# Linear attention and a gated convolution feed-forward: a new order of instructions, with two convolutions moved to VectorE and one addition made by a transfer

## The chip, the cores and the metric

The kernel runs on one core of a Trainium2 chip. The metric is the device time of one execution in microseconds. The engines are TensorE (PE, with its weight loads PEld), VectorE (DVE), ScalarE (ACT), GpSimd (POOL) and SyncE (SP). Each has its own instruction queue, which runs in order, and they meet in semaphores. Loads are issued by POOL, SP and ACT and carried out by 16 DMA engines.

## The reference, cut to what matters

For 8 batches, 8 heads, 576 positions and head size 64:

```
kv   = k^T v                            # per head, 64 x 64
o    = q kv
x    = o / sqrt(mean(o^2) + 1e-6) * g   # per head; heads side by side: x is 576 x 512
h    = max(x w_in, 0)                   # 576 x 1024
c    = w[0] * h[s-1] + w[1] * h[s] + w[2] * h[s+1]   # along the sequence, per channel
out  = (h * sigmoid(c)) w_out           # 576 x 512, fp32
```

All inputs are fp32. The kernel works in bf16 with fp32 accumulation.

## The kernel before, in words

The kernel is one list of tokens, `ORDER`. Each token names a small operation and its arguments, and behind `@` the buffers that it takes: a PSUM bank (0 to 7, two neighbours for most), or a slot of a ring in SBUF. A loop at the end runs the tokens in turn, and a last pass ties every instruction to the one before it on its engine. So the list fixes, for each engine, the order of all its work; a token that waits holds up everything behind it on the same engine. The list was written out by a planner, with costs for the operations.

Tokens by engine, with arguments `b` (batch), `u` (half of the heads, 4 each), `s` (half of the sequence), `f` (one of 8 groups of 128 hidden channels):

- Loads: `pre` brings batch 0's q, k, v in fp32 into staging buffers, by SP and ACT, in the order of `HEAD`. All other loads are on POOL's queue and cast to bf16 on the way: `Li` (w_in), `Lo` (w_out), `Lq`, `Lk`, `Lv` (one batch, or half of one where the last argument is 2). `gt` makes POOL wait for one staged tile of k before the first of them. q has three slots, k and v two; a load into a slot waits for the last reader of the batch that had it.
- Head: `cad` and `caa` cast the staged tiles on DVE and ACT; `ps`, `pl`, `pn`, `pg`, `pc`, `dg` and `ct` make constants (a spreading matrix, a selection matrix, the scaled convolution weights, and diagonal matrices of them). `fi` issues unread products of zeros on TensorE, `n` of `w` columns.
- Attention: `kv` (k^T v, L402; for batches 6 and 7 `kz`, L479), its copy `kva` on ACT or `kvd` on DVE; `qt` (transposes of q, L433) and the copies `qa`, `qd`; `ot` (q kv, L460); `sq` (squares, ACT), `on` or `oq` (sums over a head with a matrix of ones: `on` in whole matmuls, `oq` in quarters), `nl` (1/sqrt, ACT), `mo` (the scaled x, DVE). Batches 4 to 7 take another way: `oc`, `ss`, `ln`, `sl`, `sp`, `mu`; batches 6 and 7 have q transposed by DMA (`tq`).
- Hidden layer: `hk` (in two parts, L658), `hs` (L628) and `hm` (L613) multiply x by w_in; `rp`, `rh` and `re` apply the maximum with zero on ACT.
- Convolution and gate: `ta` scales a channel group by the outer two weights into the buffer `taps` (two `TENSOR_SCALAR`, L681 and L682, one written one element further right), `aa` adds the two with their shifts (L687), `ab` adds h (L692), all on DVE; the middle weight has been divided out and comes back as the scale of `sg`, the sigmoid on ACT (L698). `mg` multiplies h by it (DVE, L722). The second argument is the number of batches handled at once, the third a pair of channel groups `j` (f = 2j and 2j + 1). There are two `taps` buffers. For four channel groups of batch 0 (f = 0 to 3) TensorE makes the convolution instead: `cv` is six matmuls with the identity and two diagonal matrices from `dg` (L708), and `sc` the sigmoid from PSUM (L715).
- Output: `om` multiplies h by w_out for 128 rows of a pair of batches (L732, in two parts of four matmuls), `ea` (ACT, L738) or `ed` (DVE, L743) copies the row block out of PSUM and `st` stores it (SP, L748). The last block goes in two halves (`oh`, `eh`, `sh`).

Batches go in pairs through the convolution and the output product: pair p has batches 2p and 2p + 1.

Of the kernel before, what the change touches and what calls it, by code (L numbers as in the profile page):

```python
# [64 lines left out]
sq.0.1.1@3 oq.0.0.1@0 nl.0.0.1@2 fi.1.512@4 fi.1.512@4 hk.0.1.0.0@4 hk.0.1.0.1 rp.1.0@0 on.0.1.1@0 nl.0.1.1@3
hk.0.2.0.0@5 hk.0.2.0.1 rp.2.0 dg.3 mo.0.0.1 dg.2 hk.0.3.0.0@4 hk.0.3.0.1 hk.0.0.0.0@2 hk.0.0.0.1 rp.0.0 hk.0.0.1.0@3
rp.3.0 hk.0.1.1.0@5 hk.0.3.1.0@0 mo.0.1.1 hk.0.3.1.1 rp.3.1 hk.0.1.1.1 rp.1.1 hk.0.0.1.1 rp.0.1 dg.0 hk.0.2.1.0@1
hk.0.2.1.1 qt.1.0.0@6 kv.1.0.1@4 rp.2.1 cv.0.2@2 sc.0.2@0 cv.0.3@0 qd.1.0.0@2 kvd.1.0.1@1 ot.1.0.1@6 sc.0.3 pl
sq.1.0.1@4 cv.0.1@4 cv.0.0@2 Lq.1.2.2 Lk.1.2.2 Lv.1.2.2 sc.0.1@1 fi.2.512@0 qt.1.1.0@0 qd.1.1.0@3 mg.0.1.1 Lo.0.8
sc.0.0 mg.0.1.0 oq.1.0.1@4 nl.1.0.1@4 mo.1.0.1@1 fi.1.512@2 hk.0.5.1.0@2 hk.0.5.0.0@3 hk.0.5.0.1 rp.5.0 hk.0.5.1.1  # L70
rp.5.1 ta.0.1.5@0 hk.0.4.1.0@0 hk.0.4.1.1 rp.4.1 hk.0.7.0.0@1 hk.0.7.0.1 kv.1.1.1@4 kvd.1.1.1 rp.7.0 ot.1.0.0@2
sq.1.0.0@5 hk.0.7.1.0@6 hk.0.7.1.1 rp.7.1 ta.0.1.7@1 ot.1.1.1@0 sq.1.1.1@6 oq.1.0.0@4 nl.1.0.0@5 mo.1.0.0 hk.0.4.0.0@6
hk.0.4.0.1 rp.4.0 hk.0.6.1.0@7 hk.0.6.1.1 rp.6.1 oq.1.1.1@4 nl.1.1.1@6 mo.1.1.1 hk.0.6.0.0@6 Lq.2.0.4@2 hk.0.6.0.1
rp.6.0 ta.0.1.4 hk.1.6.1.0@7 ta.0.1.6 hk.1.0.1.0@2 ot.1.1.0@4 sq.1.1.0@7 aa.0.1.2 hk.1.1.1.0@3 hk.1.2.1.0@6 hk.1.6.1.1
# [5 lines left out]
Lq.3.0.4@0 Lk.3.0.4@0 Lv.3.0.4@1 Lq.4.0.4@1 aa.1.1.0 hk.1.4.0.0@3 om.0.1.0.4@2 rh.1.4.1 hk.1.4.0.1 rh.1.4.0  # L80
om.0.2.0.4@5 kv.2.0.2@6 mg.0.1.3 om.0.1.4.4 ab.1.1.0 sg.1.1.0 sg.1.1.1 kvd.2.0.2@2 ot.2.0.1@0 sq.2.0.1@0 ed.0.1@0
st.0.1 qt.3.1.0@6 qd.3.1.0@1 Lk.4.0.4@1 Lv.4.0.4@0 Lq.5.0.4@2 om.0.2.4.4 on.2.0.1@2 qt.3.0.0@6 qd.3.0.0@2 nl.2.0.1@8
mo.2.0.1@2 om.0.3.0.4@4 ea.0.2@1 ot.2.1.1@6 ot.2.1.0@2 mg.1.1.0 om.0.3.4.4 ed.0.3@2 sq.2.1.0@1 sq.2.1.1@2 on.2.1.0@0
nl.2.1.0@9 mo.2.1.0 om.0.0.0.4@5 hk.1.3.0.0@4 on.2.1.1@0 st.0.2 nl.2.1.1@0 mo.2.1.1 om.0.0.4.4 ed.0.0@3 ot.2.0.0@2
# [46 lines left out]
mg.7.1.3 om.3.3.0.4@2 om.3.3.4.4 ed.3.3@5 st.3.3 mg.7.1.2 om.3.1.0.4@1 om.3.2.0.4@7 om.3.0.4.4 om.3.2.4.4 ed.3.2@0  # L131
st.3.2 ed.3.0@2 st.3.0 om.3.1.4.4 ea.3.1@1 st.3.1 om.3.4.0.4@0 om.3.5.0.4@4 om.3.6.0.4@3 om.3.7.0.4@6 om.3.7.4.4
ed.3.7@4 om.3.5.4.4 ea.3.5@3 st.3.5 om.3.4.4.4 ed.3.4@5 st.3.4 st.3.7 om.3.6.4.4 ea.3.6@0 st.3.6 oh.3.8.1@1 eh.3.8.1@2
sh.3.8.1 oh.3.8.0@0 eh.3.8.0@1 sh.3.8.0
"""


@with_exitstack
def kernel(
# [79 lines left out]
    def bank():  # L219
        return banks[:, slots.pop(0), :]  # L220
# [604 lines left out]
```

## Time and profile before

| what | value |
|---|---|
| median of 3 runs | 177.75 us (177.67 to 177.93) |
| span of the profiled execution | 175.6 us |
| median of the runs less that span | 2.15 us |
| PE busy | 167.9 us (96%) |
| DVE busy | 149.5 us (85%) |
| ACT busy | 148.9 us (85%) |
| POOL busy | 22.2 us (13%) |
| moved by DMA | 29.11 MB |

The profiled execution is told by its span, from its first to its last instruction; of its own time nothing else is given, so the table sets the span beside the median of the runs. Some time before and after the span belongs to a run as well. The page lists busy times by engine, forty slices of the span with the busy share of each engine, the chain of work that ended last, and groups of instructions by source line. A landing time is counted from the issue of a transfer.

### The profile page before, as it was taken

The numbers are of one execution on the slowest core, as the hardware profiler recorded it, in microseconds if no ns is written. First come the engines' busy times: TensorE is split into PE (matmuls) and PEld (weight loads), VectorE is DVE, ScalarE is ACT, GpSimd is POOL, SyncE is SP. The second block draws the span as 40 slices with busy tenths as digits, with TensorE's granted clock in tenths as the row PEclk, the third lists the DMA queues.
The fourth block names the chain that finished last, engine by engine and source line by source line (L and its number), as shares of the span: only waits on it lengthen the run. The fifth ranks groups of instructions, "written<-read, shape, count | busy, mean of one in ns | idle before, by whom it ended". The sixth has DMA issues, their size and how long they took to land.

```text
span 175.6 us, 5070 instructions
## 1 busy us (share of the span) xinstructions
PE 167.9 (96%) x2097; PEld 100.0 (57%) x2114; DVE 149.5 (85%) x290; ACT 148.9 (85%) x268; POOL 22.2 (13%) x35
## 2 busy tenths in 40 slices
PE   7979999999999999999999999999999999999992
PEld 2334766676447677644467764444877744444451
DVE  2796638899688899999999998989999999999950
ACT  2368899999978999999999998999999967676721
POOL 3094512200603013030000000000000000000000
PEclk9999999999999999999999999999999999999999
DMA  5999999999999999999999050330310003064486
GB/s 159 392 323 207 207 207 207 208 208 209 207 241 230 227 207 207 170 182 197 258 181 161 14 134 0 119 123 0 119 63 0 0 0 116 13 239 175 179 304 237
DMA packets 25911, 29.11 MB, mean 166 GB/s; under 512 B 6036, under 2 KB 20384, under 8 KB 25888
## 3 DMA queue, kind: packets, MB, share of 16 engines
q0 software_dynamic: 13296, 14.50, 49.2%
q1 hardware_dynamic: 12048, 13.11, 26.2%
q10 hardware_dynamic: 544, 1.18, 1.7%
q8 instruction: 16, 0.26, 0.6%
q14 instruction: 7, 0.06, 0.1%
HBM read 32.52 MB, written 9.44 MB: 239 GB/s over the span
## 4 chain that ended last, share of the span: by engine, by line
PE 76%; DVE 12%; ACT 5%; DMA 3%; issue 3%; ACTq 0%; DVEq 0%
PE banks L732 32%; PE banks L628 14%; PE banks L613 9%; PE banks L658 4%; DMA stg<-in_v_dram 3%; PE banks L460 3%; DVE h L722 2%; PE banks L708 2%; ACT taps L698 2%; PE banks L402 2%; PE banks L593 2%; PE banks L433 1%; PE banks L528 1%; DVE taps L681 1%; PE banks L286 1%
## 5 line engine op out<-in xcount | busy, mean ns | idle before, releaser
L732 PE MATMUL banks<-w_out_sb,h 128*128 128x512 bf16 x267 | 62.8, 379 | 1.2 <-issue 0.6
L698 ACT ACTIVATE taps<-taps,cw 128x576 bf16<-128x576 bf16 (+1 forms) x44 | 40.6, 958 | 5.7 <-DVE taps L692 5.5
L732 PEld LDWEIGHTS <-h 128*128 128x128 bf16 x280 | 26.2, 98 | 30.0 <-issue 1.1
L628 PE MATMUL banks<-x,w_in_sb 128*128 128x288 bf16 (+2 forms) x256 | 34.2, 286 | 0.0
L640 ACT ACTIVATE h<-banks 128x288 bf16<-128x288 f32 (+2 forms) x80 | 29.5, 460 | 0.3 <-PE banks L658 0.2
L628 PEld LDWEIGHTS <-w_in_sb 128*128 128x128 bf16 x256 | 24.4, 98 | 7.8 <-issue 0.8
L722 DVE TENSOR_TENSOR h<-h,taps 128x1152 bf16<-128x1152 bf16 (+1 forms) x24 | 22.8, 952 | 1.2 <-ACT taps L698 1.2
L687 DVE TENSOR_TENSOR taps<-taps 128x1152 bf16<-128x1152 bf16 (+1 forms) x22 | 21.5, 978 | 0.5
L509 ACT ACTIVATE sq<-banks 128x576 bf16<-128x576 f32 (+2 forms) x32 | 20.8, 691 | 1.1 <-PE banks L460 1.1
L692 DVE TENSOR_TENSOR taps<-taps,h 128x1152 bf16<-128x1152 bf16 (+1 forms) x22 | 21.4, 972 | 0.3
L681 DVE TENSOR_SCALAR taps<-h,cw 128x576 bf16<-128x576 bf16 (+1 forms) x44 | 18.7, 424 | 0.6 <-ACT h L665 0.5
L682 DVE TENSOR_SCALAR taps<-h,cw 128x576 bf16<-128x576 bf16 (+1 forms) x44 | 18.4, 418 | 0.0
L738 ACT ACTIVATE row<-banks 128x512 f32<-128x512 f32 x23 | 13.5, 597 | 5.7 <-PE banks L732 4.2
L658 PE MATMUL banks<-x,w_in_sb 128*128 128x288 bf16 (+2 forms) x128 | 17.7, 286 | 0.1
L613 PE MATMUL banks<-x,w_in_sb 128*128 128x288 bf16 x128 | 16.9, 286 | 0.0
L556 DVE SCALAR_TENSOR_TENSOR x<-banks,cw,rs 128x576 bf16<-128x576 f32 (+2 forms) x16 | 13.0, 816 | 3.9 <-ACT rs L545 3.6
L658 PEld LDWEIGHTS <-w_in_sb 128*128 128x128 bf16 x128 | 12.0, 98 | 4.4 <-issue 0.5
L227 ACT ACT_TABLE_LOAD x10 | 12.8, 1283 | 2.0 <-issue 1.8
L613 PEld LDWEIGHTS <-w_in_sb 128*128 128x128 bf16 x128 | 12.3, 98 | 3.7 <-issue 0.2
L443 DVE COPY qT<-banks 128x1152 bf16<-128x1152 bf16 (+2 forms) x13 | 8.8, 681 | 5.7 <-PE banks L433 5.7
L545 ACT ACTIVATE rs<-banks,eps_sb 128x576 f32<-128x576 f32 (+2 forms) x16 | 11.8, 740 | 1.1 <-PE banks L528 1.1
L599 DVE SCALAR_TENSOR_TENSOR x<-o,cw,banks 128x576 bf16<-128x576 f32 (+2 forms) x16 | 12.1, 810 | 0.7 <-PE banks L593 0.5
(89 smaller groups left out, 162.9 us busy)
## 6 DMA issues: line engine op xcount, KB each, us to landing
out_dram<-row SPq DMA_DIRECT2D x35, 256.0 KB, 2.3
q_sb<-in_q_dram POOLq DMA_DIRECT2D x6, 576.0 KB, 17.9
k_sb<-in_k_dram POOLq DMA_DIRECT2D x6, 576.0 KB, 14.5
v_sb<-in_v_dram POOLq DMA_DIRECT2D x6, 576.0 KB, 17.9
stg<-in_v_dram ACTq DMA_DIRECT2D x2, 576.0 KB, 6.2
stg<-in_k_dram SPq DMA_DIRECT2D x4, 288.0 KB, 6.9
w_in_sb<-in_moe_w_in_dram POOLq DMA_DIRECT2D x2, 512.0 KB, 9.9
w_out_sb<-in_moe_w_out_dram POOLq DMA_DIRECT2D x1, 1024.0 KB, 15.5
```

Source lines behind the costliest of these rows:

```text
L509: nc.scalar.activation(T["sq", b, u, s], T["o", b, u, s], AX.Square)
L613: nc.tensor.matmul(ps[:, s, :HS], w_in_sb[:, t, f * P:(f + 1) * P], T["x", b][:, t, c0:c1], start=(t == 0), stop=(t == NT - 1))
L628: nc.tensor.matmul(ps, w_in_sb[:, t, f * P:(f + 1) * P], T["x", b][:, t, c0:c1], start=(t == 0), stop=(t == NT - 1))
L640: nc.scalar.activation(h, fr, AX.Relu)
L658: nc.tensor.matmul(T[at], w_in_sb[:, t, f * P:(f + 1) * P], T["x", b][:, t, c0:c1], start=(t == 0), stop=(t == NT - 1))
L681: nc.vector.tensor_scalar_mul(tap[:, 0, f % 2, :n, 8:8 + S], h[:, f], cw[:, f:f + 1])
L682: nc.vector.tensor_scalar_mul(tap[:, 1, f % 2, :n, :S], h[:, f], cw[:, 2 * NF + f:2 * NF + f + 1])
L687: nc.vector.tensor_add(tap[:, 1, :, :n, :S], tap[:, 0, :, :n, 7:7 + S], tap[:, 1, :, :n, 1:1 + S])
L692: nc.vector.tensor_add(y, y, span(b, n)[:, 2 * j:2 * j + 2])
L698: nc.scalar.activation(y, y, AX.Sigmoid, scale=cw[:, NF + f:NF + f + 1])
L722: nc.vector.tensor_mul(h, h, tap_of(b, j)[:, 1, :, :n, :S])
L732: nc.tensor.matmul(T["om", p, m], h[:, f, m * P:(m + 1) * P], w_out_sb[:, f, :], start=(f == 0), stop=(f == NF - 1))
```

## The change

The whole list `ORDER` is replaced by another. What differs in it, and in the functions:

- Two of the four `cv`, for f = 2 and 3 of batch 0, are gone with their `sc` and the builds `dg.2` and `dg.3`; the same channel groups go by `ta.0.1.2`, `ta.0.1.3`, `aa.0.1.1`, `ab.0.1.1`, `sg.0.1.2`, `sg.0.1.3`.
- `ad.4.2.2` takes the place of `aa.4.2.2` (batches 4 and 5, channel groups 4 and 5): a transfer issued by POOL adds the second tap to the first in place, so the sum stands in the other half of the buffer, at column 7. `y_of` hands that place to `ab`, `sg` and `mg`, and `mg` then sets the padding column to zero again.
- The unread products of the start are now `ff`, in fp32 (9 of 256 columns, and five of 128, 192 or 256 behind or between them), with fewer and narrower `fi` behind them.
- The head: four casts go from DVE to ACT (eight are on ACT, four on DVE), `pn`, `pl`, `ps` come early, `HEAD` brings k of the last heads ahead of `q.1.0`, and w_in is loaded in three parts instead of two.
- POOL's loads stand in another order: all of w_in first, then batch 1, batch 2, w_out, batch 3, then q4, k4, q5, v4, v5, q6, k5, v6, q7, k6, v7, k7. Before it was: half of w_in, half of batch 1, the rest of w_in, the rest of batch 1, w_out, batch 2, batch 3, q4, k4, v4, q5, q6, k5, v5, q7, k6, v6, k7, v7.
- Five `on` become `oq`, three `kvd` become `kva` and one `kva` a `kvd`, one `qd` becomes `qa`; six `ed` become `ea` and six `ea` become `ed`, and one `eh` becomes `dh`.
- Work of all engines is put in other places, and into other banks and slots: `kv.4.0.2`, for one, stands ahead of eight `hs` and three `qt` that it used to follow.

The functions that are new or changed, and the parts of the new list that this text speaks of:

```diff
+... Lv.1.0.2@1 ... Lq.1.0.2@1 ... Lk.1.0.2@0 ... Lq.1.2.2 ... Lv.1.2.2 ... Lk.1.2.2
+... Lq.2.0.4@0 ... Lk.2.0.4@1 ... Lv.2.0.4@0 ... Lo.0.8 ... Lq.3.0.4@2 ... Lv.3.0.4@1 ... Lk.3.0.4@0 ... Lq.4.0.4@1
+... kv.2.0.2@6 hk.1.7.0.1 om.0.1.0.4@2 Lk.4.0.4@1 ... Lq.5.0.4@0 ... Lv.4.0.4@0 ...
+hs.2.7.1@2 nl.3.1.0@1 hs.2.6.0@3 mo.3.1.0 kv.4.0.2@4 qt.4.0.0@6 kvd.4.0.2@0 qt.5.0.0@0 sg.1.1.5 Lv.6.0.4@0 qd.4.0.0@0
...
+    def pair(n):
+        if 2 * n <= 512:
+            return bank()[:, :2 * n].rearrange("p (e n) -> p e n", e=2)
+        return bank2()[:, :, :n]
...
-    HEAD = (("sync", "q.0.0 k.0.1 k.1.1 q.1.0 k.2.1 k.3.1 q.0.1 q.1.1"), ("scalar", "v.0.2 v.2.2"))
+    HEAD = (("sync", "q.0.0 k.0.1 k.1.1 k.2.1 k.3.1 q.1.0 q.0.1 q.1.1"), ("scalar", "v.0.2 v.2.2"))
...
+    @op
+    def ff(n, w):
+        ps, z = bank(), zero.bitcast(FP32)
+        for _ in range(n):
+            nc.tensor.matmul(ps[:, :w], z[:, :P], z[:, :w], start=True, stop=True)
...
     def on(b, u, s):
-        ps = T["on", b, u, s] = bank2()[:, :, :c1 - c0]
+        ps = T["on", b, u, s] = pair(c1 - c0)
...
+    @op
+    def ad(b, n, j):
+        tap = tap_of(b, j)
+        T["y", b, j] = tap[:, 0, :, :n, 7:7 + S]
+        nc.gpsimd.dma_start(out=T["y", b, j], in_=tap[:, 1, :, :n, 1:1 + S], accum_op=AL.add)
+
+    def y_of(b, n, j):
+        if ("y", b, j) not in T:
+            T["y", b, j] = tap_of(b, j)[:, 1, :, :n, :S]
+        return T["y", b, j]
...
     def mg(b, n, j):
         h = span(b, n)[:, 2 * j:2 * j + 2]
-        nc.vector.tensor_mul(h, h, tap_of(b, j)[:, 1, :, :n, :S])
+        nc.vector.tensor_mul(h, h, y_of(b, n, j))
+        if ADS & {(b, j)}:
+            nc.vector.memset(tap_of(b, j)[:, 0, :, :n, 7:8], 0.0)
```

More of the change, by code (lines that the diff above doesn't have):

```diff
@@ L65 @@
[L65 to L74, printed above, removed]
@@ L80 @@
[L80 to L84, printed above, removed]
@@ L408, in kvc @@
     def kvc(eng, b, u0, n):
-        if u0 == 0:
+        if ("kvb", b) not in T:
             T["kvb", b] = ring("kvb", [P, 2, 2 * D], BF16, "kvb")
@@ L437, in qc @@
     def qc(eng, b, u, s):
-        if s == 0:
+        if ("qT", b, u) not in T:
             T["qT", b, u] = ring("qT", [P, 2, S], BF16, "qT")
```

141 lines of the change are left out of this document (78 added, 63 removed).

## The prediction

> **What bounds the kernel now.** I read the page first: busy shares, slices, chain.
>
> ```profile
> span 175.6 us, 5070 instructions
> ...
> PE 167.9 (96%) x2097; PEld 100.0 (57%) x2114; DVE 149.5 (85%) x290; ACT 148.9 (85%) x268; POOL 22.2 (13%) x35
> ...
> DMA  5999999999999999999999050330310003064486
> GB/s 159 392 323 207 207 207 207 208 208 209 207 241 230 227 207 207 170 182 197 258 181 161 14 134 0 119 123 0 119 63 0 0 0 116 13 239 175 179 304 237
> ...
> PE 76%; DVE 12%; ACT 5%; DMA 3%; issue 3%; ACTq 0%; DVEq 0%
> ```
>
> TensorE is busy for 96% and carries 76% of the chain, so at first sight less TensorE work is less time. But the DMA row shows a second full resource: the 16 engines are at nine tenths or more from slice 2 to slice 22 (4.4 to about 92 us), at a flat 207 GB/s through most of it. That is the stream of loads that also casts q, k, v and both weights to bf16, all issued on POOL. [...]
>
> Next I asked for the stretches, then the issue and landing of single loads.
>
> ```profile
> 12.90:27.10 14.20, 13.57 (x245) 8.83 (x247) 7.98 (x25) 12.95 (x23) 5.55 (x8) 1.00 1.22 207
> ...
> 32.40:40.90 8.50, 8.50 (x139) 6.50 (x137) 7.90 (x16) 8.09 (x18) 0.00 (x0) 1.00 1.21 208
> ```
>
> (Columns: window, length, busy time and count of PE, PEld, DVE, ACT, POOL, granted clock, DMA, GB/s.) The rate is the same in both, and ACT is busy for 8.09 of 8.50 us in the second.
>
> The w_out load, then v of batch 2, q of batch 3, v of batch 4 and q of batch 5, each with its issue time (after the durations) and its time to landing:
>
> ```profile
> L365 POOL DMA_DIRECT2D w_out_sb<-in_moe_w_out_dram x1: 912/912/912, 16.9 to 16.9; - x1
> ...
> DMA to landing us min/median/max: 15.5/15.5/15.5
> ```
>
> ```profile
> L347 POOL DMA_DIRECT2D v_sb<-in_v_dram x1: 740/740/740, 20.8 to 20.8; - x1
> ...
> DMA to landing us min/median/max: 20.1/20.1/20.1
> ```
>
> ```profile
> L347 POOL DMA_DIRECT2D q_sb<-in_q_dram x1: 740/740/740, 23.7 to 23.7; - x1
> ...
> DMA to landing us min/median/max: 20.1/20.1/20.1
> ```
>
> ```profile
> L347 POOL DMA_DIRECT2D v_sb<-in_v_dram x1: 760/760/760, 45.0 to 45.0; - x1
> ...
> DMA to landing us min/median/max: 15.2/15.2/15.2
> ```
>
> ```profile
> L347 POOL DMA_DIRECT2D q_sb<-in_q_dram x1: 770/770/770, 45.7 to 45.7; - x1
> ...
> DMA to landing us min/median/max: 17.3/17.3/17.3
> ```
>
> Landings: w_out 32.4, v2 40.9, q3 43.8, v4 60.2, q5 63.0. They come in the order of issue. One whole-batch load takes 2.85 us of the stream (40.9 to 43.8; 60.2 to 63.0). Between v2 and v4 lie six loads (q3, k3, v3, q4, k4, v4) and the stores of three output rows:
>
> ```profile
> 45.67 7.92 SPq L748 DMA_DIRECT2D out_dram<-row  x3
> ```
>
> 19.3 us less 6 x 2.85 leaves 2.2 us, 0.72 us a row. Now who uses these loads, from TensorE's timeline:
>
> ```profile
> 16.86 0.60 PE L658 MATMUL banks<-x,w_in_sb 128*128 128x256 bf16 x4
> ...
> 41.10 1.03 PE L732 MATMUL banks<-w_out_sb,h 128*128 128x512 bf16 x3
> ```
>
> ```profile
> 63.57 0.80 PE L433 MATMUL banks<-ident,q_sb 64*64 64x64 bf16 x72
> 64.30 2.62 PE L628 MATMUL banks<-x,w_in_sb 128*128 128x288 bf16 x20
> 66.86 0.78 PE L402 MATMUL banks<-v_sb,k_sb 64*64 64x64 bf16 x72
> 67.56 4.13 PE L628 MATMUL banks<-x,w_in_sb 128*128 128x288 bf16 x32
> ```
>
> The first hidden product (`hk`) starts at 16.9, the first output product (`om.0.1`) at 41.1, 8.7 us after w_out; batch 4's k'v (`kv.4.0.2`) at 66.9, 6.7 us after v4; `qt.5.0.0` (in the 72 transposes at 63.6) only about 1 us after q5. So no load stops TensorE before, though some are close.
>
> **The change part by part.** Prices of TensorE work, from the chain in order of time:
>
> ```profile
> 22.05 1.59 PE banks L708 x12
> ...
> 25.47 0.22 PE banks L286
> ...
> 122.98 2.94 PE banks L628 x24
> ```
>
> Two convolutions cost 1.59 us, an unread 512-column product 0.22, one hidden half-product (`hs`, four matmuls) 2.94/6 = 0.49; a `qt` of a whole unit (36 transposes) is half of 64.30 - 63.57, 0.36; a whole `kv` is 67.56 - 66.86, 0.70.
>
> *Head.* The order of the fp32 head loads (k before q.1.0), four casts moved from DVE to ACT, the fp32 unread products and the new places of `ps`, `pn`, `pl`, `pc` all act before the first `hk`. Two casts no longer wait behind `ps` on DVE, but `q.1.0` comes two transfers later. Bounds for the first `hk`: 1 us earlier (both gains kept) to 2 us later; I take 0.4 earlier, 16.4, since the chain there already alternates between casts and their users and only one link shortens. An unread product of the head in the cold stage:
>
> ```profile
> 1.20 4.45 PE L286 MATMUL banks<-zero 128*128 128x512 bf16 x10 [1.20 <-DVE zero L265]
> ...
> 5.83 2.12 PE L286 MATMUL banks<-zero 128*128 128x512 bf16 x9
> ```
>
> 10 take 4.45 us (0.43 each), later 9 take 2.12 (0.22): the array starts at half rate, though the granted clock reads 1.00. [...] If it stays slow one stretch longer, the head loses up to 2 us, which is the late bound. [...]
>
> *First `hk` to first `om`.* Before it takes 41.1 - 16.9 = 24.2 us. Gone are two convolutions (1.59) and three unread products (0.65); `kv.2.0.2` and half an `hk` are moved ahead of the `om` (0.95). That gives 22.95 us, so TensorE could start `om.0.1` at 39.4. VectorE gets the two convolutions instead (four `ta`, `aa`, `ab`), about 2.5 us:
>
> ```profile
> L687 DVE TENSOR_TENSOR taps<-taps 128x1152 bf16<-128x1152 bf16 x14 | 10.6, 759 | 0.3
> L692 DVE TENSOR_TENSOR taps<-taps,h 128x1152 bf16<-128x1152 bf16 x14 | 10.5, 753 | 0.1
> L681 DVE TENSOR_SCALAR taps<-h,cw 128x576 bf16<-128x576 bf16 x28 | 10.4, 373 | 0.6 <-ACT h L665 0.5
> ```
>
> DVE is busy 7.98 of 14.2 us in the window 12.9 to 27.1, and four `dg` builds of diagonals go, so this is covered there. ScalarE keeps its count (two `sc` become two `sg`).
>
> *But the loads.* POOL's order changes: q, k, v of batch 2 now stand ahead of w_out. The set of bytes up to w_out is then the one that before ended with v2, so w_out lands at 40.9 instead of 32.4, and `om.0.1` waits from 39.4 to 40.9. The whole gain so far is gone: it starts 0.2 earlier than before. A first `hk` anywhere up to 17.9 gives the same, so the head's bounds don't reach the end.
>
> *First `om` to `kv.4`.* Before this takes 66.9 - 41.1 = 25.8 us. In the new order eight `hs` (3.9) and three `qt` of batches 4 and 5 (1.1) stand behind `kv.4`, one `hs` (0.5) and the 0.95 above ahead: 25.8 - 5.0 - 0.95 + 0.5 = 20.3. TensorE would reach `kv.4.0.2` at 61.2. But q5 now stands ahead of v4 in POOL's order, and four output rows are stored early instead of three. v4: 40.9 + 7 x 2.85 + 4 x 0.72 = 63.7. Bounds: 63.0 (fourth row hidden) and 64.5 (loads that the POOL issues later). TensorE is in order: behind `kv.4` stand the `qt` and `hs` that it used to run there; DVE's next is the copy `kvd.4`, ACT has only a few sigmoids. I take a wait of 2.5 us, to 63.7.
>
> *After `kv.4`.* It starts 3.2 us earlier than before (66.9 to 63.7), but 5.0 - 0.5 = 4.5 us of TensorE work that used to be done is still to do: +1.3 us. After this point nothing of TensorE's work is removed. The copies of output rows: six `ed` become `ea` and six `ea` become `ed`, an even trade between DVE and ACT. I put it at 0, bounds -0.8 and +1.5, because DVE and ACT are both busy nearly all the time there (4.65 and 4.92 of 5 us in the row below), so that small shifts can open or close gaps of TensorE:
>
> ```profile
> 125.00:130.00 5.00, 5.00 (x45) 3.83 (x44) 4.65 (x6) 4.92 (x12) 0.00 (x0) 1.00 0.42 157
> ```
>
> *The accumulating transfer.* It replaces one of these on DVE and adds a small memset; the next addition then reads and writes at column 7:
>
> ```profile
> L687 DVE TENSOR_TENSOR taps<-taps 128x2304 bf16<-128x2304 bf16 x8 | 10.9, 1361 | 0.2
> L692 DVE TENSOR_TENSOR taps<-taps,h 128x2304 bf16<-128x2304 bf16 x8 | 10.8, 1355 | 0.2
> ```
>
> DVE saves 1.3 us. No row shows such a transfer: from below a 256 KB store (2.3 us), from above a 576 KB load in the full stream (17.9):
>
> ```profile
> out_dram<-row SPq DMA_DIRECT2D x35, 256.0 KB, 2.3
> q_sb<-in_q_dram POOLq DMA_DIRECT2D x6, 576.0 KB, 17.9
> ```
>
> Around 105 us the engines are almost idle, so nearer the store: about 6 us for 576 KB read twice and written once. Between `ad` and the `ab.4.2.2` that needs it DVE has `mg`, two `ta`, `aa`, `ab` and two `ed`, about 7 us. So 0; were it the upper end, DVE would stop some 10 us with `sl.6` behind it. The aligned and the odd addition cost 1355 and 1361 ns: odd reads are free. [...]
>
> **Sum.** 0 (head) + 0 (first `om`, absorbed) - 3.2 + 4.5 + 0 + 0 = +1.3 us: span 176.9. The page gives the span alone; the median 177.75 stands 2.15 us above it, which I carry over: 179.05, say 179.0.
>
> **Rivals.**
> *The loads are not the bound* (faster). If w_out and v4 are there in time, TensorE starts `om` at 39.4 and `kv.4` at 59.7: 7.2 earlier, 4.5 more to do, -2.7: 175.1. With v4 alone early, `kv.4` at 61.2, -1.2: 176.6. It decides at v4 landing at 62.4 (66.9 - 4.5): earlier is faster. For it: margins of 1 us are usual in this kernel, and my 63.7 is only 1.3 above. Against: the flat 207 GB/s and landings in order of issue.
> *The wait is made good* (no change). The stop lets ACT finish sigmoids, and later gaps of DVE, spared 1.3 us, close by about 1 us: 177.8.
> *More waits than this one* (slower still). ACT has nine `rh` and four `sg` more behind `kv.4` than before, one `ea` and one `eh` fewer:
>
> ```profile
> L698 ACT ACTIVATE taps<-taps,cw 128x576 bf16<-128x576 bf16 x28 | 20.7, 777 | 5.6 <-DVE taps L692 5.5
> ...
> L640 ACT ACTIVATE h<-banks 128x288 bf16<-128x288 f32 x48 | 17.1, 428 | 0.2 <-PE banks L658 0.2
> ...
> L738 ACT ACTIVATE row<-banks 128x512 f32<-128x512 f32 x23 | 13.5, 597 | 5.7 <-PE banks L732 4.2 <-issue 1.4
> ```
>
> 9 x 0.43 + 4 x 0.78 - 2 x 0.6 is 5.8 us, 1.3 more than TensorE's 4.5; with the transfer late by as much, 2.5 us more: 181.5. For it: ACT's full windows; against: a stopped TensorE lets ACT work ahead on sigmoids that are ready.
>
> **How the numbers follow.** Forecast (v4's wait decides, 178.2 to 180.3) 0.55; more waits 0.20; made good 0.08; faster 0.17. Within 0.2% (about what can be told from no change) means 177.4 to 178.1. Faster 0.17, same 0.08, slower 0.75. The range leaves out the clearly faster end (0.12) and the worst (0.08): 176.9 to 181.8. The forecast's own range is 178.2 to 180.3.
>
> **What would show it.** The DMA row still full to slice 21; w_out landing near 40.9 and v4 near 63.7; in the waits, TensorE (PEld L402) for `v_sb` of some 2 us and for `w_out_sb` of about 1 us, which the page before lacks; DVE's `kvd` late with it. The first `hk` near 16.4 and L708 at half its count. `ab.4.2.2` not waiting for the transfer. Wrong if v4 lands before 62.4, or if TensorE comes to `kv.4` after 64 for other reasons.

## The result, and the profile after

The changed kernel takes 182.43 us (median of 4 runs, 181.89 to 184.29) against 177.84 for the kernel before on the same chip: 1.0271 times the time, with a 95% interval from 1.0219 to 1.0323. The forecast was 179.0. The profiled execution took 181.89 with a span of 180.1, so 1.8 us lie around the span (2.15 before). The executions of several kernels with long stops of TensorE scatter by 2 us and more (181.89 to 184.29 here, 181.04 to 187.41 in e9 below), the long ones mostly at a lower mean TensorE clock (184.29 at 0.991 here, 185.87 to 187.41 at 0.97 to 0.98 in e9), so profiles at a mean clock of 1.00 are compared where this matters.

The page of the changed kernel:

```profile
span 180.1 us, 5092 instructions
...
PE 168.5 (94%) x2111; PEld 102.1 (57%) x2111; DVE 149.2 (83%) x286; ACT 153.0 (85%) x274; POOL 24.2 (13%) x37
...
PE   7799988999799995999999999999999999999992
...
DMA  5999999999999999999999204883110003435334
...
q8 instruction: 16, 0.26, 0.6%
...
PE 74%; ACT 13%; issue 4%; DVE 4%; DMA 3%; POOL 0%; ACTq 0%; DVEq 0%; POOLq 0%
```

TensorE has no less work, ACT has 4 us more and 13% of the chain instead of 5%. The PE row has a hole that the one before did not: a 5 in the sixteenth slice (67.5 to 72 us). The row `q8 instruction` was on the page before too, and I had not read it: 16 packets of 16 KB of instructions. I take them to be TensorE's: its 2111 weight loads and 2111 products make some 264 a packet, and in the seven kernels below that give TensorE 56 to 260 instructions more the row has 17 packets, in all others 16.

The landings of w_out and of batch 4's v (issue time behind the durations, then time to landing):

```profile
L377 POOL DMA_DIRECT2D w_out_sb<-in_moe_w_out_dram x1: 884/884/884, 21.9 to 21.9; - x1
...
DMA to landing us min/median/max: 19.2/19.2/19.2
```

```profile
L359 POOL DMA_DIRECT2D v_sb<-in_v_dram x1: 770/770/770, 44.4 to 44.4; - x1
...
DMA to landing us min/median/max: 19.7/19.7/19.7
```

They land at 41.1 and 64.1 (forecast 40.9 and 63.7). But TensorE waits for neither. Its timeline at the steps of the prediction (start, duration, operation; in brackets the idle time before and what ended it):

```profile
16.66 1.05 PE L670 MATMUL banks<-x,w_in_sb 128*128 128x256 bf16 x8
...
42.87 2.75 PE L757 MATMUL banks<-w_out_sb,h 128*128 128x512 bf16 x12
...
45.70 0.59 PE L445 MATMUL banks<-ident,q_sb 64*64 64x64 bf16 x49
47.52 0.38 PE L445 MATMUL banks<-ident,q_sb 64*64 64x64 bf16 x23 [1.24 <-issue]
...
64.67 0.78 PE L414 MATMUL banks<-v_sb,k_sb 64*64 64x64 bf16 x72
65.26 0.84 PE L445 MATMUL banks<-ident,q_sb 64*64 64x64 bf16 x72
66.03 2.38 PE L640 MATMUL banks<-x,w_in_sb 128*128 128x288 bf16 x18
70.52 1.89 PE L640 MATMUL banks<-x,w_in_sb 128*128 128x288 bf16 x14 [2.11 <-issue]
```

The first `hk` comes at 16.66, the first `om` at 42.87 (41.10 before), `kv.4` at 64.67 (66.86 before). Twice TensorE stops in the middle of an operation: 49 transposes into a pair of `qt` of 36 each, and 18 products into a row of `hs`, the fifth of which has done two of its four products. A bank that is not ready would stop an operation at its first instruction, not there; and the other half of x, which the third product of an `hs` is the first to read, VectorE had finished by 65.3. "issue" means that the profile shows nothing it waited for. The kernel before has no such stop of a quarter microsecond or more.

So `kv.4` comes 2.2 us earlier, 4.5 us of moved work stand behind it (eight `hs` and three `qt` more, one `hs` fewer, at the prices of the prediction), and there is a stop of 2.1 us: 4.4 of the 4.5 us by which the span grew.

### The profile page after: what moved, and what is told of

Its sections match the earlier page's. It is cut to its first block, busy times and chain, and to the rows that moved or that the text cites. A ratio compares the mean times of both kernels' runs of the same rounds, so it can differ in the third digit from the quotient of the medians.

```text
span 180.1 us, 5092 instructions
## 1 busy us (share of the span) xinstructions
PE 168.5 (94%) x2111; PEld 102.1 (57%) x2111; DVE 149.2 (83%) x286; ACT 153.0 (85%) x274; POOL 24.2 (13%) x37
## 4 chain that ended last, share of the span: by engine, by line
PE 74%; ACT 13%; issue 4%; DVE 4%; DMA 3%; POOL 0%; ACTq 0%; DVEq 0%; POOLq 0%
PE banks L757 30%; PE banks L640 15%; PE banks L625 9%; PE banks L670 7%; DMA cw_rows<-in_g_norm_dram 3%; ACT sq L521 3%; ACT L232 3%; PE banks L472 2%; ACT rs L557 2%; PE banks L445 2%; PE banks L549 2%; PE banks L414 2%; ACT h L652 2%; DVE x L611 1%; ACT h L677 1%
## 5 line engine op out<-in xcount | busy, mean ns | idle before, releaser
L757 PE MATMUL banks<-w_out_sb,h 128*128 128x512 bf16 x280 | 64.2, 379 | 0.0
L721 ACT ACTIVATE taps<-taps,cw 128x576 bf16<-128x576 bf16 (+1 forms) x46 | 42.6, 953 | 3.5 <-DVE taps L715 3.5
L640 PE MATMUL banks<-x,w_in_sb 128*128 128x288 bf16 (+2 forms) x256 | 34.5, 286 | 2.1 <-issue 2.1
L640 PEld LDWEIGHTS <-w_in_sb 128*128 128x128 bf16 x256 | 24.1, 98 | 10.6 <-issue 3.5
L715 DVE TENSOR_TENSOR taps<-taps,h 128x1152 bf16<-128x1152 bf16 (+1 forms) x23 | 22.1, 961 | 0.3
L699 DVE TENSOR_TENSOR taps<-taps 128x1152 bf16<-128x1152 bf16 (+1 forms) x22 | 20.9, 948 | 0.4
L521 ACT ACTIVATE sq<-banks 128x576 bf16<-128x576 f32 (+2 forms) x32 | 20.2, 669 | 1.0 <-PE banks L472 1.0
L693 DVE TENSOR_SCALAR taps<-h,cw 128x576 bf16<-128x576 bf16 (+1 forms) x46 | 19.3, 419 | 1.7 <-ACT h L677 1.3
L694 DVE TENSOR_SCALAR taps<-h,cw 128x576 bf16<-128x576 bf16 (+1 forms) x46 | 19.6, 427 | 0.0
L670 PE MATMUL banks<-x,w_in_sb 128*128 128x288 bf16 (+2 forms) x128 | 18.2, 287 | 0.0
L625 PEld LDWEIGHTS <-w_in_sb 128*128 128x128 bf16 x128 | 12.2, 98 | 4.6 <-issue 0.7
L557 ACT ACTIVATE rs<-banks,eps_sb 128x576 f32<-128x576 f32 (+2 forms) x16 | 11.9, 743 | 3.1 <-DVE taps L693 1.2
L670 PEld LDWEIGHTS <-w_in_sb 128*128 128x128 bf16 x128 | 11.6, 98 | 4.7 <-issue 1.4
L768 DVE COPY row<-banks 128x512 f32<-128x512 f32 x12 | 8.2, 685 | 4.7 <-PE banks L757 4.6
```

Of the source, the lines that this page charges most:

```text
L521: nc.scalar.activation(T["sq", b, u, s], T["o", b, u, s], AX.Square)
L625: nc.tensor.matmul(ps[:, s, :HS], w_in_sb[:, t, f * P:(f + 1) * P], T["x", b][:, t, c0:c1], start=(t == 0), stop=(t == NT - 1))
L640: nc.tensor.matmul(ps, w_in_sb[:, t, f * P:(f + 1) * P], T["x", b][:, t, c0:c1], start=(t == 0), stop=(t == NT - 1))
L670: nc.tensor.matmul(T[at], w_in_sb[:, t, f * P:(f + 1) * P], T["x", b][:, t, c0:c1], start=(t == 0), stop=(t == NT - 1))
L693: nc.vector.tensor_scalar_mul(tap[:, 0, f % 2, :n, 8:8 + S], h[:, f], cw[:, f:f + 1])
L694: nc.vector.tensor_scalar_mul(tap[:, 1, f % 2, :n, :S], h[:, f], cw[:, 2 * NF + f:2 * NF + f + 1])
```

## The experiments

Two theories for the stops were set against each other. A: TensorE runs out of instructions. They come in blocks through a DMA queue of their own (q8 on the page, 16 packets of 16 KB), beside the full stream of loads, and a block of short instructions is used up before the next is there. B: the stops come from data, banks or other engines in the new order. Other questions were whether the loads hold TensorE as forecast, and what the two named parts do alone. The kernels are called by the first part of their labels, e1 to e16.

### More short instructions in the kernel before (e1, e2)

`fk.n` is a new token: n unread products of zeros, 64 by 64, so two short instructions each.

```diff
-fi.9.512@0
+fi.4.512@0 fk.104@0
```

> The kernel before, with five of nine unread 512-column products of the cold head replaced by 104 unread 64x64 products, so that TensorE has about 198 more short instructions and the same work there. Their results are read by nobody. Theory A (the two stops in mid-operation, 1.24 us at 46.3 and 2.11 us at 68.4 of the changed kernel, are TensorE waiting for its own instructions, which come in blocks by a DMA queue that the full load stream slows down): the same short, dense work now meets block borders as the changed kernel's does, so stops of about 2 us open near 47 and near 67 us, and the kernel before gets 2 to 4 us slower. Rival B (the stops come from data, banks or engines of the changed order): nothing moves, within 0.5 us.

Measured: 1.0338 times the kernel before (1.0281 to 1.0396), 184.3 us. The stops in its TensorE timeline:

```profile
13.75 0.32 PE L409 MATMUL banks<-v_sb,k_sb 64*64 64x64 bf16 x16 [0.94 <-issue]
...
49.36 0.28 PE L440 MATMUL banks<-ident,q_sb 64*64 64x64 bf16 x10 [1.06 <-issue]
...
72.03 0.35 PE L409 MATMUL banks<-v_sb,k_sb 64*64 64x64 bf16 x21 [2.03 <-issue]
...
82.07 0.59 PE L409 MATMUL banks<-v_sb,k_sb 64*64 64x64 bf16 x49 [1.55 <-issue]
```

Two of them stand near the places foretold, 2.4 and 5 us later and 1.06 and 2.03 us long; two more came beside them. Nothing of the order behind the head was touched: the old order gets the same kind of stops once its instructions are counted from another start. Between the last two the trace holds 127 matmuls and 127 weight loads, so some 256 instructions, one packet. That distance comes back below (126 and 128 in e3, 127 and 128 in e16). The stops add up to 5.6 of the 7.9 us by which this span grew; the clock granted from 72 to 82 us was 0.83, and 32 products of `hs` took 5.77 us there (4.09 in e3).

The control had 56 instructions more:

```diff
-fi.9.512@0
+fi.7.512@0 fk.30@0
```

> The control of the other: two of the nine unread products become 30 short ones, 56 more instructions. Both theories: no stop opens (theory A: the block borders then fall into slower stretches, total stops about 0.1 us), time within 0.5 us of the kernel before. If this one gets slower too, it is the short products in the head, not the place of the borders.

Measured: 180.88 us, 1.0141 (1.0095 to 1.0187). The expectation failed: two stops opened, one of them in the head, where I had not worked out where the borders fall.

```profile
16.05 0.46 PE L467 MATMUL banks<-qT,kvb 64*64 64x320 bf16 x5 [0.72 <-issue]
...
79.24 0.60 PE L739 MATMUL banks<-w_out_sb,h 128*128 128x512 bf16 x2 [0.56 <-issue]
```

They are of the kind that A calls for and in mid-operation, but this run shows that A foretells the place of a stop better than its absence. With its 1.3 us of stops it accounts for less than half of the 3.3 us by which this span grew; of the rest, 1.5 us arose at the very end, where copies of rows waited for stores.

What settles the place is the count of weight loads ahead of each stop. The profile of the changed kernel up to its second stop, and that of the old order without two convolutions (e5 below) up to its stop in the middle of `kv.4` (TensorE and its weight loads are the first two counts):

```profile
0.00:70.00 70.00, 62.75 (x1117) 40.87 (x1117) 53.15 (x133) 60.06 (x113) 19.67 (x32) 1.00 1.16 229
```

```profile
0.00:70.00 70.00, 63.58 (x1109) 39.11 (x1117) 53.21 (x137) 56.80 (x108) 19.31 (x31) 1.00 1.15 228
```

| weight loads before the stop | kernels |
|---|---|
| 223 | e1, e2, e9, e12 |
| 734 | changed, e4, e7, e8, e10, e14 |
| 862 | e1 |
| 1117 | changed, e4, e5, e7, e8, e10, e11, e13, e14 |
| 1245 | e1, e3, e9, e12, e16 |
| 1372 or 1373 | e1, e2, e3, e10, e12, e13, e16 |

These are all the stops that the profiles put down to "issue" and that last 0.4 us or more, with those of e7, e10 and e13 that bear VectorE's name (below) and three shorter ones at the same counts. The counts lie 128 apart, or multiples of that to within one, in both orders, whatever operation stands there and whatever data come when. Theory B gives no reason for that.

### Short instructions in the quiet and in the stream (e15, e16)

The sharpest test of A came last. The same 130 short products, once at 100 us, where the loads are over, and once at 72 us.

```diff
-om.1.2.0.4@2
+fk.130@2 om.1.2.0.4@2
```

> The kernel before with 260 short unread instructions (130 products of 64x64, 2.1 us of TensorE by the 82 that took 1.32 us in an earlier run) ahead of om.1.2.0.4 at 100 us, where the loads are over. If the stops come from the instruction supply behind a full load stream: at most a small stop here (under 1 us), span 2 to 3 us longer. If a block of 256 short instructions stalls anywhere: a stop of some 3.5 us, as in the stream.

```diff
-om.0.7.0.4@2
+fk.130@2 om.0.7.0.4@2
```

> The same 260 short instructions ahead of om.0.7.0.4 at 72 us, inside the load stream. Instruction supply: a block takes about 5.6 us from one border to the next there (41.9 to 47.5 and 64.9 to 70.5 in the changed kernel), these would use one up in 2.1 us, so stops of 3 to 4 us at or right behind them, marked as issue, span 5 to 7 us longer. If stops have nothing to do with it: 2.1 us longer and no stop.

Measured: 179.01 us in the quiet (1.0077), 185.89 in the stream (1.0464). TensorE's timelines, quiet first:

```profile
100.39 1.26 PE L293 MATMUL banks<-zero 64*64 64x64 bf16 x130
```

```profile
72.21 0.23 PE L293 MATMUL banks<-zero 64*64 64x64 bf16 x6
73.15 1.20 PE L293 MATMUL banks<-zero 64*64 64x64 bf16 x124 [0.72 <-issue]
...
79.62 1.12 PE L635 MATMUL banks<-x,w_in_sb 128*128 128x288 bf16 x4 [4.30 <-issue]
```

Same instructions, same engine: 1.3 us and no stop where the DMA engines are lightly used (share 0.38 from 100 to 102 us); 5.0 us of stops where they are full (share 1.28 from 75 to 79 us). Between the two stops lie 127 matmuls and 128 weight loads. That settles A against "short instructions as such". From the first stop's end to the second's it is 6.5 us, about what one packet takes through the full stream (my 5.6 was from two cases). The stream run then also lost clock: the mean granted to it from 80 to 84 us was 0.50 (columns as in the prediction):

```profile
80.00:84.00 4.00, 3.67 (x87) 1.86 (x85) 1.79 (x3) 2.75 (x5) 1.48 (x2) 0.50 0.75 126
```

### Moving the borders in the changed kernel (e3, e9, e10)

```diff
-ff.3.256@2 ff.1.128@2
+ff.2.256@2 fk.82@2
```

> The changed kernel with about 154 more short unread instructions in the head in place of one and a half of its long unread ones, the same TensorE work. Theory A: the block borders move out of the dense stretches, the stops of 1.24 and 2.11 us shrink to about 0.6 us in all, and the time falls by up to 2 us, to 180.3 or so (the first, at 46 us, lies where ScalarE is full and may give nothing; the second, behind kv.4, should give its 2 us). Rival B: no change, within 0.5 us.

Measured: 183.85 us, 1.0321 (1.0259 to 1.0383): no gain. Yet both stops are gone. What is left, and what came (the last row is from the waits):

```profile
71.23 0.54 PE L452 MATMUL banks<-ident,q_sb 64*64 64x64 bf16 x40 [0.58 <-issue]
...
77.26 0.35 PE L421 MATMUL banks<-v_sb,k_sb 64*64 64x64 bf16 x21 [0.41 <-issue]
```

```profile
PE banks L519 <- DMA qT<-q_sb: 2.6, 1, 2.6
```

`om.0.7` came at 74.65 instead of 76.17, and then TensorE stood 2.6 us for `tq.6.0`, the transposing transfer for batch 6, which had taken 17.8 us to land (13.0 in the changed kernel). A stop was removed and a transfer became the wait. So two more kernels, both with that transfer issued early and with the head filled (next part), one with the borders moved and one without:

```diff
-ff.4.256@0 ... tq.6.1@4 ... tq.6.0@0
+ff.5.256@0 ... tq.6.1@4 tq.6.0@5 ...
```

> The changed kernel with the head filled (five fp32 products), the block borders moved by about 154 short instructions, and the transposing transfer tq.6.0 issued right behind tq.6.1 (at about 71 instead of 78 us, into a buffer of its own), since in the run with moved borders it landed 17.8 us after issue and TensorE waited 2.6 us for it. Theory (the stop of 2.1 to 2.6 us behind kv.4 is TensorE's instruction supply and costs its length once nothing else is late): stops of at most 1.0 us in all, no wait for tq.6.0, time 1.5 to 2.5 us below the filled head alone (181.9), so 179.4 to 180.4. Rival (the time comes back at another wait anyway): 181.3 or more.

> The same without the moved borders: filled head and early tq.6.0. Its place in the order alone should do nothing, as no wait for it shows in the profile with the filled head: 181.9 within 0.5 us, the stop of some 2.5 us near 68 us still there. If this one is as fast as the one with moved borders, the borders are not the cause.

Measured: e10 182.51 us, 1.0250 (1.0213 to 1.0287). e9's four executions lie between 181.04 and 187.41, so that their median, 186.08, says nothing; the profiled one took 181.04, which is above the expected range, and still waits 0.67 us for `tq.6.0`, which was to be gone. e10's two executions at a mean clock of 1.00 took 181.28 and 182.75, so what the moved borders gain lies between 0.2 and 1.7 us, by one execution of e9. The stops of e9, then three rows of e10:

```profile
14.35 0.41 PE L292 MATMUL banks<-zero 128*128 128x512 bf16 x2 [1.55 <-issue]
...
71.57 0.55 PE L452 MATMUL banks<-ident,q_sb 64*64 64x64 bf16 x42 [0.62 <-issue]
```

```profile
64.04 0.77 PE L414 MATMUL banks<-v_sb,k_sb 64*64 64x64 bf16 x72 [1.05 <-DMA v_sb<-in_v_dram]
...
70.08 2.13 PE L640 MATMUL banks<-x,w_in_sb 128*128 128x288 bf16 x16 [2.55 <-DVE taps L715]
...
86.95 0.65 PE L578 MATMUL banks<-sq,sel 128*32 128x288 bf16 x13 [1.71 <-issue]
```

In e9 the big stop behind `kv.4` is gone and a new one stands in the head. From `kv.4` to `om.0.7` it takes 10.0 us, against 11.9 in e10 and 11.5 in the changed kernel. In e10 the stop is named "DVE taps L715". This name is not the cause: 1117 weight loads stand before it, as in the changed kernel. The fifth fp32 product in the head has moved the border two matmuls ahead in the order, so the row before the stop has 16 matmuls, four whole `hs`; the stop falls between two operations, and the profile takes the engine that ended last. What the fifth `hs` needs is the bank that a copy of DVE had freed by 66.6:

```profile
65.22 1.41 DVE L455 COPY qT<-banks 128x1152 bf16<-128x1152 bf16 x2
```

Do stops reach the end? For the profiles at full clock, take how much `kv.4` moved against the kernel before, 4.5 us of moved work (where the order is the changed one), and the stops behind `kv.4`:

| kernel | `kv.4` | moved | stops behind | sum | span less 175.6 |
|---|---|---|---|---|---|
| changed | -2.2 | 4.5 | 2.1 | 4.4 | 4.5 |
| e7, head filled | -2.8 | 4.5 | 2.6 | 4.3 | 3.9 |
| e8, relu on DVE | -2.0 | 4.5 | 2.3 | 4.9 | 4.7 |
| e9 | -1.9 | 4.5 | 0.6 | 3.3 | 3.6 |
| e10 | -2.8 | 4.5 | 4.3 | 5.9 | 5.3 |
| e5, convolutions alone | 2.2 | 0 | 1.0 | 3.1 | 3.4 |
| e11, sigmoids in another order | 1.9 | 0 | 1.0 | 2.9 | 3.6 |
| e2, 56 instructions more | 1.1 | 0 | 0.6 | 1.7 | 3.3 |

The sums hold within 0.7 us, but for e2, where 1.5 us arose at the very end (above). Stops behind `kv.4` go to the end for the greater part: from e9 to e10 they grow by 3.7 us, and what the span has beyond `kv.4` and the moved work by 2.6. No run took the stop of 2.1 us away and left all else as it was, so its price at the end is worked out from this table and not measured by itself.

### The head (e7)

```diff
-ff.4.256@0
+ff.5.256@0
```

> The changed kernel with five instead of four fp32 unread products ahead of the first transposes, which closes a gap of TensorE of 0.9 to 1.1 us (4.7 to 5.8 us). Theory (this gap decides whether the array falls back to half rate: the eight products behind the transposes took 1.78 us in the changed kernel's profile, 3.35 us in that of the run with v4 first): they take 1.8 us in this profile, first hk near 16.7, median 0.3 to 1.0 us below the changed kernel's 182.4 and less spread. Rival: the head's lateness is not from the gap or is made good later: no change, within 0.3 us. The two stops at 46 and 68 us stay in both.

Measured: 181.89 us, 1.0221 (1.0172 to 1.0271), against 1.0271 for the changed kernel: 0.5 us less, inside both intervals, so a hint and no more. The eight products took 2.11 us, not 1.8, with the first `hk` at 16.39; of the two stops that were to stay, the second did (2.55 us), the first shrank to 0.30. The head's cold stretch is plain in single profiles. The fp32 products behind the first transposes, in the changed kernel and in e3, whose head is the same up to there:

```profile
6.05 1.78 PE L298 MATMUL banks<-zero 128*128 128x256 f32 x8
```

```profile
6.21 2.07 PE L298 MATMUL banks<-zero 128*128 128x256 f32 x4
```

The first row's eight are six of 256 columns and two of 128. From start to start a product of 256 columns takes 0.22 us in the one and 0.43 in the other, after a gap of 1.13 and of 0.88 us. In the first the prediction's bound of one more half-rate stretch was not taken up, in the second it was. The longer gap stands ahead of the faster row. With the gap closed by the fifth product the eight took 2.11 us in e7's profile and 1.78 in that of e13, whose head is the same. What decides between the two rates is not shown.

### Does v4 hold `kv.4`? (e4, e13, e12)

```diff
-Lq.5.0.4@0 ... Lv.4.0.4@0
+Lv.4.0.4@0 ... Lq.5.0.4@0
```

> The changed kernel with v of batch 4 loaded ahead of q of batch 5 again, as before the change. The prediction's step (v4, landing at 63.7, is what holds kv.4): v4 lands 2.9 us earlier and the time falls by 1 to 2.5 us. The new reading (TensorE comes to kv.4 at 64.7 for other reasons and v4, at 64.1, is there): kv.4 moves by less than 0.5 us, the time within 0.5 us, unless the transposes of q5 right behind it now wait, which would show as a wait for q_sb at L445.

Measured: 1.0234 (1.0166 to 1.0302), the same as the changed kernel within the intervals; its waits name neither v_sb nor q_sb for TensorE at `kv.4`. But in its profile the head was at half rate for longer (3.35 us, above), and TensorE came to `kv.4` only at 65.80, so this run alone proves little. In the changed kernel as it is, v4 landed 0.6 us before TensorE came, and did not matter. With the filled head TensorE came earlier, and the forecast wait appeared: 0.54 us in e7, 1.05 in e10 (row above), with `kv.4` pinned at 64.1 and 64.0. So the swap was made again there, and together with moved borders:

> The changed kernel with the filled head and the early tq.6.0 (where kv.4 started at 64.04 after a wait of 1.05 us for v4), and v of batch 4 ahead of q of batch 5 again. Prediction's step (v4 holds kv.4): the wait goes, kv.4 starts near 63.0. Its transposes of q5 then wait for q5, which lands at 64 or so: some 0.4 us. Of the 1.0 us, 0.3 to 1.0 reaches the end if the stops behind kv.4 (2.55 and 1.71 us) keep their length. Rival: kv.4 stays at 64.0, something else holds it.

> As the first of this set, with v of batch 4 ahead of q of batch 5 again. Prediction's step (kv.4 waits for v4): with the stop at 46 us gone TensorE should reach kv.4 near 63.2 to 63.5 while v4 lands at 64, so this wait of 0.5 to 0.8 us, hidden until now, shows in the first of this set and goes here; the time falls by 0.3 to 0.8 us unless q5, now 2.9 us later, holds the transposes behind kv.4 (a wait for q_sb at the transposes' line). Rival (v4 never matters): within 0.2 us and no wait for v_sb in either.

Measured for e13: 182.52 us, 1.0261 (1.0240 to 1.0281), no gain over e10. Its timeline and two windows:

```profile
62.95 0.78 PE L414 MATMUL banks<-v_sb,k_sb 64*64 64x64 bf16 x72
...
68.84 2.99 PE L640 MATMUL banks<-x,w_in_sb 128*128 128x288 bf16 x16 [2.32 <-DVE taps L699]
```

```profile
66.00:70.00 4.00, 1.68 (x15) 1.13 (x13) 2.95 (x7) 1.83 (x6) 0.00 (x0) 0.99 1.21 208
70.00:74.00 4.00, 4.00 (x92) 2.76 (x90) 1.18 (x2) 2.96 (x8) 0.99 (x2) 0.58 1.32 205
```

`kv.4` starts 1.09 us earlier and waits for nothing, so v4 was what held it there. The gain did not last: the stop came all the same, and the clock behind it fell to 0.58 for four microseconds, which cost the next sixteen products 0.86 us (2.99 against 2.13 in e10). e12 tells nothing on v4: `kv.4` came at 65.0 as in e9, too late for the wait, and a k load (1.9 us) and a transposing transfer (0.3 us) came to be waited for instead; its times scatter from 180.3 to 187.0.

### Does w_out hold the first `om`? (e14)

```diff
-Lq.2.0.4@0 ... Lv.2.0.4@0 ... Lo.0.8
+Lo.0.8 Lq.2.0.4@0 ... Lv.2.0.4@0 ...
```

> The changed kernel with w_out loaded ahead of batch 2 again: it lands near 32.5 instead of 41.1, v2 still near 41. Prediction's step (the first om waits for w_out): the first om up to 1.5 us earlier than 42.9. New reading (batch 1's norms on ScalarE set it, w_out is there): first om within 0.3 us of 42.9 beside the head's own shift, time within 0.7 us of 182.4, kv.2.0.2 right ahead of it not waiting.

Measured: 183.89 us, 1.0356 (1.0340 to 1.0371), 1.5 us slower. w_out lands at 32.4, and the first `om` comes at 46.3, 3.4 us later. Neither side expected that. 2.1 us of it is this wait:

```profile
PE banks L445 <- DMA q_sb<-in_q_dram: 2.1, 1, 2.1
```

Behind it the granted clock fell to 0.64 and 0.50 from 36 to 40 us, and a row of eighteen `hk` products took 4.05 us instead of 2.38, which covers the rest. The new order transposes batch 2's q at 33.2 (36.2 before the change), and with w_out ahead q2 lands at 35.3. So the swapped loads, which I had booked as the loss of the whole gain, are needed by the new order and cost nothing at the first `om`.

### The two named parts alone, and ScalarE's chain (e5, e11, e8, e6)

In the kernel before, `cv.0.2`, `cv.0.3`, their `sc` and diagonals out, and:

```diff
-... ot.1.0.1@6 ... sc.0.1@1
+... ot.1.0.1@6 ta.0.1.2@0 ta.0.1.3 aa.0.1.1 ab.0.1.1 ... sg.0.1.2 sg.0.1.3 sc.0.1@1
```

> The kernel before with the named part alone: convolutions 2 and 3 of batch 0 go from TensorE to VectorE (two ta, aa, ab behind kvd.1.0.1, sigmoids from there), their diagonals go. Prediction's step (TensorE sets the stretch from the first hk to the first om): 1.59 us less TensorE work, the first om up to 1.6 us earlier, time 0 to 1.5 us less. Rival (ScalarE sets it, busy 4.5 to 5 of 5 us from 15 to 40 us in both kernels, with two sigmoids as before): first om within 0.5 us of 41.1, no gain, and a loss of up to 2 us where the sigmoids wait for the VectorE chain. TensorE has 24 instructions fewer, so stops at block borders may move too; these are read from the trace apart.

Measured: 181.22 us, 1.0204 (1.0163 to 1.0245). 1.6 us less on TensorE, and 3.3 us slower. ACT's timeline in this run, and the first norm of batch 1 in the kernel before:

```profile
23.15 0.65 ACT L509 ACTIVATE sq<-banks 128x576 bf16<-128x576 f32 x1 [1.34 <-PE banks L460]
23.81 1.28 ACT L227 ACT_TABLE_LOAD   x1
25.46 1.44 ACT L698 ACTIVATE taps<-taps,cw 128x576 bf16<-128x576 bf16 x2 [0.37 <-DVE taps L692]
...
29.47 0.74 ACT L545 ACTIVATE rs<-banks,eps_sb 128x576 f32<-128x576 f32 x1
```

```profile
27.60 0.74 ACT L545 ACTIVATE rs<-banks,eps_sb 128x576 f32<-128x576 f32 x1
```

Before, ACT passed without a pause from the relus of batch 0 to the sigmoids of the convolutions, and then by a table load to the first norm. With the convolutions on VectorE it has nothing ready for 1.34 and 0.37 us, and the first norm comes 1.87 us later. The first `om` is late by just that: 42.94 against 41.10. So in this stretch the order of ACT's passes sets the end, not the sum of TensorE's work. A stop of 0.97 us near 70 comes on top. I then put the sigmoids of the TensorE pair first:

```diff
-sg.0.1.2 sg.0.1.3 sc.0.1@1 ... sc.0.0
+sc.0.1@1 sc.0.0 sg.0.1.2 sg.0.1.3 ...
```

> The kernel before with the two convolutions on VectorE, but with ScalarE's sigmoids of the TensorE pair (sc.0.1, sc.0.0) ahead of those of the VectorE pair. Theory (the loss of 1.84 us by the first om comes from ScalarE, which sits idle for 1.34 and 0.37 us until VectorE's chain of four products and two additions is done, with the table load and the first norm of batch 1 behind it): the idle time goes, the first norm (29.47 there, 27.60 before) comes at 28.0 to 28.5, the first om 1.0 to 1.5 us earlier than 42.94, time down by as much from 181.2. Rival (VectorE's load or the norms' own chain sets it): within 0.4 us.

Measured: 1.0236 times the kernel before (1.0182 to 1.0289); no gain.

```profile
23.30 0.65 ACT L509 ACTIVATE sq<-banks 128x576 bf16<-128x576 f32 x1 [1.34 <-PE banks L460]
...
29.27 0.74 ACT L545 ACTIVATE rs<-banks,eps_sb 128x576 f32<-128x576 f32 x1
```

The gap of 0.37 goes, the one of 1.34 stays. I had misread its row: ACT waits there for `ot.1.0.1` (L460), which the sigmoids used to cover; VectorE's chain does not end it. Sigmoids that can't start before that point cost their cover, whichever order follows.

In the changed kernel the sigmoids stand earlier, and the norm is late by 0.57 us only (28.17). With the 0.95 us of work that the new order puts ahead of the first `om` this makes 1.5 of the 1.8 us by which that `om` is late. Taking work from ACT there:

```diff
-rp.2.1 ... rp.3.1 ... rp.0.1 ... rp.1.1
+dp.2.1 ... dp.3.1 ... dp.0.1 ... dp.1.1
```

(`dp` is `rp` as a maximum with zero on VectorE.)

> The changed kernel with four relu passes of the first stretch (rp.2.1, 3.1, 0.1, 1.1; some 0.46 us each) on VectorE instead of ScalarE. Theory (from the first hk to the first om, 16.7 to 42.9 us, ScalarE sets the pace): the stretch of 26.2 us gets 1 to 1.9 us shorter, TensorE's gaps at 25 to 30 us shrink. Rival (the loads or TensorE set it): shorter by less than 0.4 us. What of it reaches the end depends on kv.4 (v4 lands at 64.1 all the same) and on the stops: 0 to 1 us.

Measured: 183.84 us, 1.0310 (1.0258 to 1.0363); the stretch from first `hk` to first `om` took 27.1 us instead of 26.2.

```profile
22.57 0.74 ACT L745 ACTIVATE taps<-banks,cw 128x576 bf16<-128x576 f32 x1 [1.55 <-PE banks L738]
```

ACT now waits 1.55 us for the convolution, which waits for the relus on VectorE. My theory that ACT's load is what counts there falls: it is a chain of relu, convolution, sigmoid, table load and norm, and moving a link makes it no shorter.

The other part alone, in the kernel before:

```diff
-ta.4.2.4@0 ... ta.4.2.5 aa.4.2.2 ab.4.2.2
+ta.4.2.4@0 ta.4.2.5 ad.4.2.2 ... ab.4.2.2
```

> The kernel before with the other named part alone: one addition of batches 4 and 5 (column 7 plus column 1) by an accumulating transfer, issued behind its two ta, and the memset behind its merge. Prediction's step: VectorE saves 1.3 us, the transfer lands in about 6 us, nothing waits: time within 0.4 us of before. Rival (a transfer late by 10 us or a slow odd write costs it): 1 us or more slower, with ab.4.2.2 waiting for the transfer.

Measured: 177.80 us over 10 runs, 0.9996 (0.9977 to 1.0014). The transfer costs nothing and gives nothing.

## Why the prediction was wrong, point by point

The direction was right, the size wrong by 3.4 us on the median. In the profiled execution it was 2.8 us (181.89 against 179.05): `kv.4` 1.0 us later than forecast, 2.1 us of stop, 0.35 less around the span.

- *Head*: right. First `hk` at 16.66, forecast 16.4. The bound of 2 us for a second cold stretch was taken up in e4's profile (the eight products took 3.35 us instead of 1.78), not in this one.
- *First `hk` to first `om`*: wrong. I took 22.95 us by subtracting TensorE's work from TensorE's stretch; it took 26.2. The row of the forecast itself had ACT busy for 8.09 of 8.50 us. The windows from 20 to 30 us, before and after:

```profile
20.00:30.00 10.00, 9.85 (x212) 6.61 (x211) 5.24 (x19) 9.70 (x17) 2.08 (x4) 1.00 1.23 207
```

```profile
20.00:30.00 10.00, 8.57 (x198) 5.87 (x197) 6.97 (x14) 9.94 (x18) 2.38 (x3) 1.00 1.21 208
```

  From 20 to 30 us TensorE is idle for 1.3 us more, and ACT stayed full.
- *But the loads* (w_out): landing right to 0.2 us, conclusion wrong. TensorE was 1.8 us behind w_out's landing, and e14 shows that the other order of loads is worse.
- *First `om` to `kv.4`*: right in size. 20.3 us forecast, 21.8 measured, of which 1.24 is the first stop.
- *v4*: landing right (64.1 for 63.7), the wait of 2.5 us not there, since TensorE came at 64.67, "for other reasons", as the prediction's last part had put it. With an earlier TensorE the wait is real (e7, e10) and goes with v4's load (e13). That `kv.4` came within 1.0 us of the forecast all the same is luck: the first `om` was 2.0 us later than forecast and the way from there 1.5 us longer, in place of the 2.5 us of waiting.
- *After `kv.4`*: the 4.5 us of moved work fit the table. The step that failed is the sum's silence on what follows, put at 0 but for the copies of rows: `kv.4` (144 instructions) and two `qt` (144) in 1.4 us use up more than a packet of instructions, and the next came 2.11 us late. In the order before, 20 products of `hs` (2.6 us) ran between the transposes and `kv.4`, and there is no such stop.
- *The accumulating transfer*: right. It landed 6.0 us after issue (forecast about 6):

```profile
L705 POOL DMA_DIRECT2D taps<-taps x1: 1542/1542/1542, 111.6 to 111.6; - x1
...
DMA to landing us min/median/max: 6.0/6.0/6.0
```

  `ab.4.2.2` began at 118.10, 0.5 us behind the landing and without a wait, and its odd write took the usual time:

```profile
118.10 1.35 DVE L715 TENSOR_TENSOR taps<-taps,h 128x2304 bf16<-128x2304 bf16 x1
```

  `ab.4.2.3` just before, which writes at column 0, took 1.36 us, so the odd write cost nothing here.
- *Copies of rows at 0*: the sum of the changed kernel in the table leaves 0.1 us for them.
- *The full stream*: it was read as ending at about 92 us; slice 22 of the page's DMA row ends at 96.6. Nothing in the sum hangs on it.
- *Rivals*: "more waits" gave 181.5 and came nearest in size, but its reason (ACT's 5.8 us against TensorE's 4.5) is not what the trace shows; the wait was in a queue that I had not looked at.

What stays open: why the clock falls after some stops and not after others; how long a packet of instructions takes in general (only 5.6 and 6.5 us between borders were seen in the full stream); and why the first stop was 1.24 us in the changed kernel and 0.30 in e7, at the same count of weight loads.

## What to carry to other kernels

Before subtracting an engine's work from a stretch, ask which engine's chain ends it: here two convolutions taken off TensorE saved 1.6 us there and cost 1.8, because the sigmoids had been covering a wait of ScalarE. Count TensorE's instructions as well as its time where transfers fill the DMA engines: some 260 short ones in a microsecond or two outran their own supply here (e16). A stop in the middle of an operation that is put down to "issue" was the sign here (1.24 and 2.11 us in the changed kernel); where it fell between two operations the profile named an engine that had nothing to do with it (2.55 us in e10). Counting the weight loads ahead of the stop told the two apart: they came to the same few numbers in every kernel (734 or 1117, say).

## What the runs showed that I had not expected

- 260 short instructions cost 1.3 us at 100 us and 5.0 us of stops besides at 72 us, inside the stream of loads.
- 56 unread instructions in the head, of no use to anybody, made the kernel 1.4% slower (1.0141).
- After a stop of 2.3 us the granted clock was 0.58 over four microseconds (e13), after one of 4.3 it was 0.50 (e16); after 2.11 us in the changed kernel's profile it stayed at 1.00, and after 2.07 us at the same place in e4's it was 0.50 from 72 to 74 us.
- A transposing transfer of the same size took 13.0 us to land in one order and 17.8 in another that issued it 1.5 us earlier.
